# A Fourier-mixing kernel: the second sequence chunk with one plain x pair instead of three, and one sum over xn made by an accumulating DMA

## The chip, the core and the metric

The kernel runs on one core of a Trainium2 chip. A core has TensorE (matmuls, called PE in the profile; PEld is its weight load), VectorE (DVE), ScalarE (ACT), GpSimd (POOL) and SyncE (SP, which here only issues DMAs). The metric is device time in microseconds of one execution: 670.5 us before the change, the median of 3 runs (669.85 to 670.7).

## The reference

x is 2048 x 512. Everything is float32.

```python
xn = _layernorm(x, axis=-1)
a = einsum("bsd,ed->bse", xn, dft_hid_re);  b = einsum("bsd,ed->bse", xn, dft_hid_im)
s = einsum("ts,bse->bte", dft_seq_re, a) - einsum("ts,bse->bte", dft_seq_im, b)
h = einsum("bsd,df->bsf", xn, w1) + b1;  h = relu(h) ** 2      # F = 1792
g = silu(einsum("bsf,fd->bsd", h, w2) + b2)
out = x + s * g
```

The change touches the product of the sequence matrices with the normalised x alone (the kernel does the sequence side first and the hidden side afterwards).

## The kernel before, in words

**Number format.** Every float32 operand is split into a high part (ScalarE copies it into TensorE's format, `split_hi`, L137) and a low part (VectorE subtracts the high part, `split_lo`, L140). A product is three matmul passes: high by high, high by low, low by high (`PASSES`).

**Seven products.** Large matrix products are done block by block as 2 x 2 blocks in seven products instead of eight (Strassen's scheme in Winograd's form). That needs sums of the blocks on both sides: of x, four sums S1 to S4; of the sequence matrix, four sums T1 to T4 (`sums_b`, L299 to L304: three VectorE instructions, 512, 256 and 256 columns wide a partition). A block of the sequence matrix then has 7 parts of 256 columns to split (1792 columns), a plain one 4 (1024).

**Staging of the first part.** The rows of x lie in 16 tiles of 128, two to a "pair" j = 0 to 7. The sequence matrix comes in column chunks of 256, c = 0 to 7; chunk c for pair j is loaded as one block, "block j", into one of three buffers `u`, split into operand `g`, which has two buffers (`ga` for even j, `gb` for odd j). Pairs of x stay in SBUF as operands `xc0` to `xc7`, seven parts each: four raw ones and S1 to S4.

- Chunk 0 goes pair by pair with plain products (`products`, L402, 24 matmuls of 512 columns a pair) while x is being normalised: mean and variance (`ln_stats`, `ln_mean`, `ln_var`), the root, and xn itself by VectorE (`ln_xn`, L242) or by ScalarE (`ln_xn_act`, L253, which needs a small `ln_shift`, L248, by VectorE first). Chunk 0's results are copied out of the PSUM banks by ScalarE (`plain_out`).
- Chunk 1 begins with the pairs of `MIXED` by eight plain products (`plain_step`, 48 matmuls of 256 columns, L391), during which the sums S over xn are formed and split; then come the pairs of `SEVEN` by seven products (42 matmuls, L391). A plain step adds into the same banks as the seven products.
- Chunks 2 to 7 use seven products for all pairs.

**The sums over xn.** `sums(g)` makes S1 to S4 for four pairs at once, in place in the tile `xn32` (L274, 1024 columns a partition each; g = 0 for pairs 0 to 3, g = 1 for 4 to 7). The last of its four steps is an addition, the others are subtractions. `split_sums(j)` then splits the four sums of one pair into `xc`: ScalarE the high part, VectorE the low one.

**The order around the change.** All engines work in the order in which the instructions are written; there is no scheduler. In the loop over seven-product steps n, behind the matmuls of step n are written: the sums of block n + 2 (`step_sums`), the split of block n + 1 (`step_split`), a pair's `split_sums` by the table `SUMS_AT`, the load of block n + 4 (`step_load`), results of the chunk before, and by the table `EARLY` pieces of later work (weights of the hidden side "d", of w1 "v", early operands "y", loads "p"). In the DMA queue of SP the block loads come in the order of use.

Of the kernel before, what the change touches and what calls it, by code (L numbers as in the profile page):

```python
# [11 lines left out]
ALU = mybir.AluOpType  # L12
# [3 lines left out]
NS, ND, NF = S // P, D // P, F // P  # L16
# [3 lines left out]
TC = 512  # L20
NTC = S // TC
WARM = 8, 5
MIXED = 4, 5, 6
SEVEN = 1, 0, 3, 2, 7
SUMS_AT = {1: 7, 2: 4, 3: 5, 5: 6}

REST = NP - 4

# [8 lines left out]


EARLY = {
# [7 lines left out]
}  # L47
LATER = {0: 1, 1: 1, 2: 1, 3: 1, 4: 1}
LATER_1 = {0: 1, 1: 2, 2: 1, 3: 1, 4: 1}
# [82 lines left out]
def fnet_gated_kernel(ctx, tc, x, xt, ct, wd, w1, w2, b1, b2, out):  # L132
# [9 lines left out]
    def split(*parts):  # L142
        split_hi(*parts)
        split_lo(*parts)
# [95 lines left out]
    def ln_xn(j, h):  # L240
        xn32_tile(j, h)
        nc.vector.tensor_scalar(xn32[j][:, h], xr[j][:, h], stats[:, 0, h, j:j + 1], stats[:, 1, h, j:j + 1],  # L242
                                op0=ALU.subtract, op1=ALU.mult)
# [25 lines left out]
    def sums(g):  # L269


        s = xn32[ND * g, "tile"].rearrange("p j h (b n) -> p j (h b) n", b=2)
        for to, a, b, op in ((3, 1, 3, ALU.subtract), (1, 1, 0, ALU.subtract), (0, 3, 0, ALU.subtract), (2, 2, 0, ALU.add)):
            nc.vector.tensor_tensor(s[:, :, to], s[:, :, a], s[:, :, b], op=op)  # L274
            yield

    def split_sums(j):
        s = xn32[j].rearrange("p h (b n) -> p (h b) n", b=2)
        split(XC[j][:, S2:S1 + 1, HI, :], XC[j][:, S2:S1 + 1, LO, :], s)
# [9 lines left out]
    def plain_parts(c, j, hs=slice(0, 2)):  # L289
        if (c, j) not in part:  # L290
            part[c, j] = operand_buf("g" + "ab"[j % 2], f"g{c}_{j}", 0 if c or j == NJ - 1 else 3 if j in TURNED else 1, (2, 4, CW))
        g, r = part[c, j], raw[c, j]
        s = slice(2 * hs.start, 2 * hs.stop)
        return g[:, HI, s], g[:, LO, s], r[:, s]
# [43 lines left out]
    def step_sums(n):  # L338
        if n < len(steps):
            u = raw[steps[n]]  # L340
            sums_b(u[:, 4:8], u)

    def step_split(n):
        if n < len(steps):
            s = steps[n]
            u = raw.pop(s)
            g = part[s] = buf("g" + "ab"[s[1] % 2], [P, 2, 7, CW], f"g{s[0]}_{s[1]}", F32R)
            split(g[:, HI], g[:, LO], u[:, 1:8])
# [48 lines left out]
    def products(j, h):  # L397

        for a_, b_ in PASSES:
            for k in range(ND):  # L400
                w = XC[j][:, RAW[h][k // 2], a_, k % 2 * P:(k % 2 + 1) * P]
                nc.tensor.matmul(accs[k], w, part[0, j][:, b_, 2 * h:2 * h + 2],  # L402
                                 start=j == 0 and h == 0 and (a_, b_) == (HI, HI),
                                 stop=j == NJ - 1 and h == 1 and (a_, b_) == (LO, HI))
# [23 lines left out]
    def go(*names):  # L428


        for v in names:
            if v[0] == "h" and int(v[1:]) >= NTC * NP:
                continue
            if v not in making:
                making[v] = makers[v[0]](int(v[1:]))
            next(making[v])
# [115 lines left out]
    split_hi(*g)  # L552
    for h in range(2):
        products(0, h)
    side = sums(0), sums(1)
    load_c(0, 3)
    load_x(4)
    for j in range(1, NJ):
        ln_rstd(j)
        if j == 1:  # L560
            ln_hi(j, 0)
            ln_shift(j)
            ln_xn_act(j, 0)
            ln_mean(j + 1, 1)
            split_lo(*plain_parts(0, j, one))
            ln_xn(j, 1)
            split_hi(*xc_parts(j, 1))
            split_lo(*xc_parts(j, 0))
            split_lo(*plain_parts(0, j, two))
        else:  # L570
            for h in range(2):
                ln_xn(j, h)
                split_hi(*xc_parts(j, h))
            split_lo(*g)
            split_lo(*xc_parts(j, 0))
        load_c(*order[j + 3])
        if j in (1, 3, 4):
            load_x({1: 5, 3: 6, 4: 7}[j])
        if j + 1 < NJ:
            ln_stats(j + 1)  # L580
            if j > 1:
                ln_mean(j + 1, 1)
            ln_var(j + 1, 1)
            ln_root(j + 1)
        split_lo(*xc_parts(j, 1))
        if j == NJ - 1:
            next(side[0])
        for h in range(2):
            products(j, h)
        g = plain_parts(*order[j + 1])  # L590
        split_hi(*g)
        if j == NJ - 1:
            next(side[0])
        if j == 2:
            nc.sync.dma_start(b1s, b1)
            nc.sync.dma_start(b2s, bcast(b2, D))
# [6 lines left out]
    def plain_out(k):  # L603
        to = plain[k // 2].rearrange("p (i m d t) -> p d m i t", i=2, m=2, d=2)[:, k % 2]
        copy(to, accs[k].rearrange("p (m i t) -> p m i t", m=2, i=2))

    def some(steps_, n):
        for _ in range(n):
            next(steps_)

    for i, j in enumerate(MIXED):
        if i == 0:
            some(side[0], 2)
            some(side[1], 1)
            split(*plain_parts(1, MIXED[1]))
            split_sums(0)
            split_sums(1)
            for k in range(ND):
                plain_out(k)
            for k in range(2):  # L620
                nc.sync.dma_start(PQD[0][:, k].rearrange("p k n -> p (k n)"), plain[k])
        elif i == 1:
            step_sums(0)
            split(*plain_parts(1, MIXED[2]))
            split_sums(2)
            some(side[1], 1)
        else:
            step_sums(1)
            some(side[1], 1)
            step_split(0)  # L630
            split_sums(3)
            go("d0")
        plain_step(j)
        load_c(*order[NJ + i + 4])

# [2 lines left out]
    for n, s in enumerate(steps):  # L638
        c, j = s
        if c > 1 and j == 0:  # L640
            ms = {}
        for k, tag in banks(c).items():
            if k not in ms:
                ms[k] = bank(tag, f"m{k}_{c}")
        g = part.pop(s)
        for p in FIRST if j == 0 and c > 1 else ORDER:
            a, b = PRODUCTS[p]
            mm(ms[p], XC[j][:, a], lambda b_: g[:, b_, b], (c > 1 and j == 0) or (not n and p in (1, 5, 6, 7)), s in LAST)
        step_sums(n + 2)
        step_split(n + 1)  # L650
        if n == 0:
            some(side[1], 1)
        elif n in SUMS_AT:
            split_sums(SUMS_AT[n])
        if n == 0:
            e = buf("e", [P, 2048], "c1")
            copy(chunk_part(e)(C22), halves(ms[Z]))
        step_load(n + 4)
        if closing:
            some(closing, (LATER_1 if c == 2 else LATER).get(j, 0))  # L660
            if j in (3, 4):
# [582 lines left out]
```

## Time and profile before

| | |
|---|---|
| median of 3 runs | 670.5 us |
| profiled execution | 669.43 us |
| its span, first to last instruction | 667.7 us |
| TensorE busy | 662.3 us (99%), 5599 matmuls |
| VectorE busy | 610.7 us (91%), 847 instructions |
| ScalarE busy | 382.1 us (57%), 516 instructions |
| GpSimd busy | 8.8 us (1%), 11 instructions |
| granted TensorE clock | 0.999 |

The span leaves out what lies around the program in one execution (669.43 against 667.7). Rows of a timeline give the start in us from the span's start, the length, engine, source line, operation, output <- inputs with shapes, and in brackets the engine's idle time before it and what ended that. Rows of groups give the count, the total busy time in us, the mean of one in ns, and the idle time ahead. Rows of windows give, behind the stretch, the busy us of PE, PEld, DVE, ACT and POOL with their instruction counts, then the clock and the share of the DMA engines. Matmul lengths overlap; what counts is the distance from one start to the next.

### The profile page before, as it was taken

What the parts mean: (1) busy time and instruction counts of PE and PEld (TensorE: products, weight loads), DVE (VectorE), ACT (ScalarE), POOL (GpSimd) and SP (SyncE); (2) the same over time, 40 slices, a digit from 0 to 9 for tenths busy, and PEclk for the clock granted to TensorE, in tenths of its full rate; (3) what the DMA queues carried; (4) which work ended last, traced back from release to release, by engine and by line L of the source; (5) the groups of instructions that cost most, each with busy time, mean ns of one, the idle gap of its engine ahead of it and who ended that gap; (6) DMA issues with size and microseconds to landing.
All of it is one profiled execution on the core that took longest, in us unless ns stands there. A gap on an engine that the chain in (4) does not pass through costs nothing.

```text
span 667.7 us, 13533 instructions
## 1 busy us (share of the span) xinstructions
PE 662.3 (99%) x5599; PEld 650.9 (97%) x5599; DVE 610.7 (91%) x847; ACT 382.1 (57%) x516; POOL 8.8 (1%) x11
## 2 busy tenths in 40 slices
PE   9999999999999999999999999999999999999997
PEld 6889999999999999999999999999999999999997
DVE  7999999999999999999999979887878889999997
ACT  6855554545545363635465357878778865454451
POOL 0000000000000000000000000000000000101010
PEclk9999999999999999999999999999999999999999
DMA  8634334858668865889588557675845866767676
GB/s 293 228 113 171 121 100 138 290 180 288 220 213 281 303 249 191 296 308 336 198 299 264 180 194 292 209 281 177 299 160 208 339 233 199 203 209 199 212 205 158
DMA packets 52605, 150.85 MB, mean 226 GB/s; under 512 B 5056, under 2 KB 19648, under 8 KB 51904
## 3 DMA queue, kind: packets, MB, share of 16 engines
q1 hardware_dynamic: 44432, 129.28, 57.7%
q10 hardware_dynamic: 6208, 18.88, 7.1%
q0 software_dynamic: 1904, 1.84, 1.9%
q8 instruction: 44, 0.72, 0.4%
q14 instruction: 17, 0.14, 0.1%
HBM read 101.98 MB, written 47.99 MB: 225 GB/s over the span
## 4 chain that ended last, share of the span: by engine, by line
PE 94%; DVE 5%; issue 1%; ACT 0%; DMA 0%; DVEq 0%
PE m L391 40%; PE m_o L909 14%; PE r_B L803 13%; PE r_A L803 9%; PE pq_b L402 5%; PE r_C L803 4%; PE r_D L803 4%; PE pq_bb L402 2%; DVE g L140 1%; PE warm L529 1%; DVE z L959 1%; DVE z L359 1%; DVE z L1159 0%; DVE hr L311 0%; DVE z L964 0%
## 5 line engine op out<-in xcount | busy, mean ns | idle before, releaser
L391 PEld LDWEIGHTS m<-g,xc 128*128 128x128 f32 x2370 | 269.0, 188 | 0.1
L391 PE MATMUL m<-g,xc 128*128 128x256 f32 x2370 | 269.1, 276 | 0.0
L137 ACT ACTIVATE g<-u 128x1792 fp32r<-128x1792 f32 (+2 forms) x65 | 102.3, 1574 | 132.7 <-PE m L391 65.2
L140 DVE TENSOR_TENSOR g<-u,g 128x1792 fp32r<-128x1792 f32 (+2 forms) x66 | 120.9, 1832 | 6.8 <-ACT g L137 6.2
L909 PE MATMUL m_o<-w,g 128*128 128x256 f32 x882 | 100.5, 276 | 0.0
L909 PEld LDWEIGHTS m_o<-w,g 128*128 128x128 f32 x882 | 100.3, 188 | 0.0
L137 ACT ACTIVATE g<-hr 128x1792 fp32r<-128x1792 f32 (+2 forms) x31 | 48.2, 1566 | 40.2 <-PE m_o L909 16.8
L803 PE MATMUL r_B<-xT,w 128*128 128x256 f32 x504 | 66.6, 276 | 0.0
L803 PEld LDWEIGHTS r_B<-xT,w 128*128 128x128 f32 x504 | 61.5, 188 | 0.0
L140 DVE TENSOR_TENSOR g<-hr,g 128x1792 fp32r<-128x1792 f32 (+2 forms) x31 | 56.7, 1838 | 2.9 <-ACT g L137 2.8
L803 PE MATMUL r_A<-xT,w 128*128 128x256 f32 x336 | 43.1, 276 | 0.0
L402 PE MATMUL pq_b<-g,xc 128*128 128x512 f32 x144 | 40.9, 391 | 0.0
L803 PEld LDWEIGHTS r_A<-xT,w 128*128 128x128 f32 x336 | 40.4, 188 | 0.2 <-DVE xT L140 0.2
L301 DVE TENSOR_TENSOR u<-u 128x512 f32<-128x512 f32 x53 | 36.3, 684 | 0.7 <-DMA u<-in_ct 0.6
L803 PE MATMUL r_B<-wdp,yg 128*128 128x256 f32 x288 | 35.8, 276 | 0.0
L803 PEld LDWEIGHTS r_B<-wdp,yg 128*128 128x128 f32 x288 | 34.1, 188 | 0.0
L909 PE MATMUL m_last<-w,g 128*128 128x256 f32 x294 | 33.5, 276 | 0.0
L909 PEld LDWEIGHTS m_last<-w,g 128*128 128x128 f32 x294 | 33.4, 188 | 0.0
L402 PEld LDWEIGHTS pq_b<-g,xc 128*128 128x128 f32 x144 | 26.8, 188 | 6.6 <-ACT g L137 0.7
L140 DVE TENSOR_TENSOR yg<-yraw,yg 128x1792 fp32r<-128x1792 f32 x13 | 26.2, 2020 | 0.6 <-ACT yg L137 0.6
L137 ACT ACTIVATE yg<-yraw 128x1792 fp32r<-128x1792 f32 x13 | 22.2, 1708 | 5.4 <-DVE yraw L315 4.5
L303 DVE TENSOR_TENSOR u<-u 128x256 f32<-128x256 f32 x53 | 22.5, 425 | 1.8
(185 smaller groups left out, 837.2 us busy)
## 6 DMA issues: line engine op xcount, KB each, us to landing
u<-in_ct SPq DMA_DIRECT2D x63, 512.0 KB, 4.1
hd<-h ACTq DMA_DIRECT2D x28, 512.0 KB, 4.4
hr<-hd SPq DMA_DIRECT2D x28, 512.0 KB, 3.8
wdp<-wdd SPq DMA_DIRECT2D x8, 896.0 KB, 7.1
yraw<-pqd SPq DMA_DIRECT2D x13, 512.0 KB, 5.2
pqd<-c SPq DMA_DIRECT2D x12, 512.0 KB, 5.2
w<-w1d SPq DMA_DIRECT2D x6, 896.0 KB, 7.8
y<-y ACTq DMA_DIRECT2D x8, 512.0 KB, 5.1
```

The costliest lines, as they stand in the source:

```text
L137: nc.scalar.activation(hi, src, AF.Copy)
L140: nc.vector.tensor_tensor(lo, src, hi.bitcast(F32), op=ALU.subtract)
L301: nc.vector.tensor_tensor(t[:, 0:2], r[:, 0:1].to_broadcast([P, 2, 256]), r[:, 1:3], op=ALU.add)
L303: nc.vector.tensor_tensor(t[:, 2], t[:, 1], r[:, 1], op=ALU.add)
L359: nc.vector.tensor_tensor(part_(to), m, part_(frm), op=op)
L391: nc.tensor.matmul(ps[:, d], w[:, a_, d * P:(d + 1) * P], halves(mv(b_)), start=first and d == 0 and (a_, b_) == (HI, HI), stop=last and ( ...
L402: nc.tensor.matmul(accs[k], w, part[0, j][:, b_, 2 * h:2 * h + 2], start=j == 0 and h == 0 and (a_, b_) == (HI, HI), stop=j == NJ - 1 and ...
L529: nc.tensor.matmul(warm, zeros[:, 0:P], zeros, start=True, stop=True)
L803: nc.tensor.matmul(self.region(REGION[k]), w, mv, start=i == 0 and k in (1, 7), stop=i == len(ops) - 1, skip_group_check=True)
L909: nc.tensor.matmul(m[:, i * 256:(i + 1) * 256], ready[n][:, a_, H_SLOT[a], i * P:(i + 1) * P], W2[p][:, b_, b], start=p == 0 and i == 0 an ...
L959: nc.vector.tensor_tensor(e[:, k, w], e[:, k, w], fin[c][k // 2][:, k % 2, w], op=ALU.mult)
```

## The change

Four things are done.

1. Chunk 1 has one plain pair (4) instead of three (4, 5, 6); pairs 5 and 6 move to the seven-product steps, which now go 1, 0, 3, 2, 5, 6, 7.
2. Of the four sums over xn, the addition is no longer a VectorE instruction but two accumulating DMAs on GpSimd's queue, SBUF to SBUF, for two pairs each (twice, for g = 0 and 1).
3. The last pair (7) is normalised by ScalarE (`ln_shift` and `ln_xn_act`) instead of VectorE.
4. The order of sums, splits and copies around this is rewritten, and the tables `SUMS_AT` and `EARLY` are renumbered.

```diff
-MIXED = 4, 5, 6
-SEVEN = 1, 0, 3, 2, 7
-SUMS_AT = {1: 7, 2: 4, 3: 5, 5: 6}
+MIXED = 4,
+SEVEN = 1, 0, 3, 2, 5, 6, 7
+SUMS_AT = {0: 3, 1: 2, 2: 5, 3: 6, 4: 7, 5: 4}
...
 EARLY = {
-    (2, 2): ("d0",), (2, 3): ("d0",), (2, 5): ("d0", "d1"), (2, 6): ("d0",), (3, 0): ("d1",), (3, 1): ("d1",),
+    (1, 2): ("d0",),
+    (2, 0): ("d0",), (2, 2): ("d0",), (2, 3): ("d0", "d1"), (2, 5): ("d0",), (2, 6): ("d1", "d1"), (3, 0): ("d1", "d2"),
...
         s = xn32[ND * g, "tile"].rearrange("p j h (b n) -> p j (h b) n", b=2)
-        for to, a, b, op in ((3, 1, 3, ALU.subtract), (1, 1, 0, ALU.subtract), (0, 3, 0, ALU.subtract), (2, 2, 0, ALU.add)):
-            nc.vector.tensor_tensor(s[:, :, to], s[:, :, a], s[:, :, b], op=op)
+        for to, a, b in ((3, 1, 3), (1, 1, 0), (0, 3, 0)):
+            nc.vector.tensor_tensor(s[:, :, to], s[:, :, a], s[:, :, b], op=ALU.subtract)
             yield
+        for q in (slice(0, 2), slice(2, 4)):
+            nc.gpsimd.dma_start(s[:, q, 2], s[:, q, 0], accum_op=ALU.add)
+        yield
...
+            if j == NJ - 1:
+                ln_shift(j)
+                next(side[0])
             for h in range(2):
-                ln_xn(j, h)
+                (ln_xn_act if j == NJ - 1 else ln_xn)(j, h)
                 split_hi(*xc_parts(j, h))
...
         if j == NJ - 1:
-            next(side[0])
+            some(side[0], 3)
         for h in range(2):
             products(j, h)
         g = plain_parts(*order[j + 1])
         split_hi(*g)
-        if j == NJ - 1:
-            next(side[0])
...
     for i, j in enumerate(MIXED):
-        if i == 0:
-            some(side[0], 2)
-            some(side[1], 1)
-            split(*plain_parts(1, MIXED[1]))
-            split_sums(0)
-            split_sums(1)
-            for k in range(ND):
-                plain_out(k)
-            for k in range(2):
-                nc.sync.dma_start(PQD[0][:, k].rearrange("p k n -> p (k n)"), plain[k])
-        elif i == 1:
-            step_sums(0)
-            split(*plain_parts(1, MIXED[2]))
-            split_sums(2)
-            some(side[1], 1)
-        else:
-            step_sums(1)
-            some(side[1], 1)
-            step_split(0)
-            split_sums(3)
-            go("d0")
+        some(side[1], 4)
+        step_sums(0)
+        step_split(0)
+        plain_out(2)
+        plain_out(0)
+        split_sums(1)
+        plain_out(1)
+        plain_out(3)
+        for k in range(2):
+            nc.sync.dma_start(PQD[0][:, k].rearrange("p k n -> p (k n)"), plain[k])
+        step_sums(1)
+        split_sums(0)
         plain_step(j)
         load_c(*order[NJ + i + 4])
...
         step_sums(n + 2)
         step_split(n + 1)
-        if n == 0:
-            some(side[1], 1)
-        elif n in SUMS_AT:
+        if n in SUMS_AT:
             split_sums(SUMS_AT[n])
```

How this moves instructions. Names: `u1_1` is block 1 of chunk 1, `g1_1` its split operand, `xc1` pair 1 of x, `xn32_0` and `xn32_4` the tiles of xn with the sums of pairs 0 to 3 and 4 to 7.

VectorE before, from the low half of block 4 (the first plain pair) to block 1's sums:

```order
L140 TENSOR_TENSOR g1_4_546<-u1_4_428,g1_4_546 128x1024
L274 TENSOR_TENSOR xn32_0_184<-xn32_0_184 128x4x256 x2
L274 TENSOR_TENSOR xn32_4_374<-xn32_4_374 128x4x256
L140 TENSOR_TENSOR g1_5_557<-u1_5_473,g1_5_557 128x1024
L140 TENSOR_TENSOR xc0_121<-xn32_0_184,xc0_121 128x4x256
L140 TENSOR_TENSOR xc1_126<-xn32_0_184,xc1_126 128x4x256
L301 TENSOR_TENSOR u1_1_550<-u1_1_550 128x512
```

and the same place now:

```order
L141 TENSOR_TENSOR g1_4_551<-u1_4_428,g1_4_551 128x1024
L275 TENSOR_TENSOR xn32_4_374<-xn32_4_374 128x4x256 x3
L305 TENSOR_TENSOR u1_1_473<-u1_1_473 128x512
L307 TENSOR_TENSOR u1_1_473<-u1_1_473 128x256
L308 TENSOR_TENSOR u1_1_473<-u1_1_473 128x256
L141 TENSOR_TENSOR g1_1_566<-u1_1_473,g1_1_566 128x1792
L141 TENSOR_TENSOR xc1_126<-xn32_0_184,xc1_126 128x4x256
```

The sums over pairs 0 to 3 have moved ahead of block 4, the three sums of pairs 4 to 7 stand together, and block 1's low half follows its own sums directly.

VectorE now, from there to the low half of block 0, the operand of the second seven-product pair:

```order
L305 TENSOR_TENSOR u1_0_520<-u1_0_520 128x512
L307 TENSOR_TENSOR u1_0_520<-u1_0_520 128x256
L308 TENSOR_TENSOR u1_0_520<-u1_0_520 128x256
L141 TENSOR_TENSOR xc0_121<-xn32_0_184,xc0_121 128x4x256
L305 TENSOR_TENSOR u1_3_554<-u1_3_554 128x512
L307 TENSOR_TENSOR u1_3_554<-u1_3_554 128x256
L308 TENSOR_TENSOR u1_3_554<-u1_3_554 128x256
L141 TENSOR_TENSOR g1_0_685<-u1_0_520,g1_0_685 128x1792
```

Between the low halves of blocks 1 and 0 there now stand two pairs' splits of sums and the sums of two blocks; before, one of each (pair 3's split and block 3's sums).

ScalarE now, from the last pair of chunk 0 to the high half of block 0 (`plain` are the copies of chunk 0's results, `pq0_bb` the bank in which the first of the seven products will add up):

```order
L254 ACTIVATE xn32_4_374<-x7_383,small_129,stats_68 128x512
L138 ACTIVATE xc7_125<-xn32_4_374 128x2x256
L138 ACTIVATE g1_4_551<-u1_4_428 128x1024
L138 ACTIVATE g1_1_566<-u1_1_473 128x1792
L148 ACTIVATE plain1_557<-pq0_bb_132 128x2x2x128
L148 ACTIVATE plain0_556<-pq0_b21_130 128x2x2x128
L138 ACTIVATE xc1_126<-xn32_0_184 128x4x256
L148 ACTIVATE plain0_556<-pq0_b32_131 128x2x2x128
L148 ACTIVATE plain1_557<-pq0_b31_133 128x2x2x128
L138 ACTIVATE xc0_121<-xn32_0_184 128x4x256
L138 ACTIVATE g1_0_685<-u1_0_520 128x1792
```

Block 1's high half comes ahead of all four copies; before, the four copies, the sums of pairs 0 and 1 and two plain blocks came ahead of it.

More of the change, by code (lines that the diff above doesn't have):

```diff
@@ L554, in fnet_gated_kernel, with some @@
         products(0, h)
+    def some(steps_, n):
+        for _ in range(n):
+            next(steps_)
     side = sums(0), sums(1)
@@ L605, in plain_out @@
         copy(to, accs[k].rearrange("p (m i t) -> p m i t", m=2, i=2))
-    def some(steps_, n):
-        for _ in range(n):
-            next(steps_)
     for i, j in enumerate(MIXED):
-        if i == 0:
-            some(side[0], 2)
-            some(side[1], 1)
-            split(*plain_parts(1, MIXED[1]))
-            split_sums(0)
-            split_sums(1)
-            for k in range(ND):
-                plain_out(k)
-            for k in range(2):
-                nc.sync.dma_start(PQD[0][:, k].rearrange("p k n -> p (k n)"), plain[k])
-        elif i == 1:
-            step_sums(0)
-            split(*plain_parts(1, MIXED[2]))
-            split_sums(2)
-            some(side[1], 1)
-        else:
-            step_sums(1)
-            some(side[1], 1)
-            step_split(0)
-            split_sums(3)
-            go("d0")
+        some(side[1], 4)
[10 more added lines that the diff above has]
+        split_sums(0)
         plain_step(j)
```

12 rows, old and new, of the table EARLY are left out of this document.

## The prediction

> **What bounds the kernel now.** I read the page first, then the list of waits on TensorE, then one window of the timeline engine by engine.
>
> ```profile
> span 667.7 us, 13533 instructions
> PE 662.3 (99%) x5599; PEld 650.9 (97%) x5599; DVE 610.7 (91%) x847; ACT 382.1 (57%) x516; POOL 8.8 (1%) x11
> L391 PE MATMUL m<-g,xc 128*128 128x256 f32 x2370 | 269.1, 276 | 0.0
> PE warm L529 <- DVE idle L525: 1.2, 1, 1.2
> 50.91 59.33 PE L391 MATMUL m<-g,xc 128*128 128x256 f32 x522
> 67.00:91.00 24.00, 24.00 (x214) 24.00 (x213) 22.59 (x26) 13.99 (x13) 0.00 (x0) 1.00 0.32 107
> ```
>
> The fourth row is the whole list of TensorE's waits: once warm it waits for nobody. The fifth is its timeline from the first product of the second chunk: 522 matmuls in one piece, so one starts every (59.33 - 0.276) / 521 = 0.1133 us. A plain pair of x has 48 of them, 5.44 us; a seven-product pair has 42, 4.76 us. The last row is the stretch after it (PE, PEld, DVE, ACT, POOL, clock): TensorE is full, and VectorE has 22.59 of 24 us. So TensorE sets the time, but only while VectorE, nearly as full, delivers. Any matmul removed is won, any late operand is lost.
>
> **What is removed.** Pairs 5 and 6 go from plain to seven products: 2 x 6 = 12 matmuls, 12 x 0.1133 = 1.36 us. That is the whole gain to be had.
>
> **What it costs VectorE.** The rows that price it (timeline of VectorE; start, length, what):
>
> ```profile
> 40.65 0.16 DVE L233 SCALAR_TENSOR_TENSOR stats<-small 128x2 f32<-128x2 f32 x1
> 40.85 1.00 DVE L242 TENSOR_SCALAR xn<-x,stats 128x512 f32<-128x512 f32 x2
> 41.77 1.22 DVE L140 TENSOR_TENSOR g<-u,g 128x1024 fp32r<-128x1024 f32 x1
> 42.90 1.29 DVE L140 TENSOR_TENSOR xc<-xn,xc 128x512 fp32r<-128x512 f32 x2
> 44.10 2.49 DVE L274 TENSOR_TENSOR xn<-xn 128x1024 f32<-128x1024 f32 x2
> 46.60 1.23 DVE L140 TENSOR_TENSOR g<-u,g 128x1024 fp32r<-128x1024 f32 x1
> 47.74 3.61 DVE L274 TENSOR_TENSOR xn<-xn 128x1024 f32<-128x1024 f32 x3
> 61.12 0.69 DVE L301 TENSOR_TENSOR u<-u 128x512 f32<-128x512 f32 x1
> 61.84 0.43 DVE L303 TENSOR_TENSOR u<-u 128x256 f32<-128x256 f32 x1
> 62.30 0.42 DVE L304 TENSOR_TENSOR u<-u 128x256 f32<-128x256 f32 x1
> 62.64 1.22 DVE L274 TENSOR_TENSOR xn<-xn 128x1024 f32<-128x1024 f32 x1
> 63.78 2.03 DVE L140 TENSOR_TENSOR g<-u,g 128x1792 fp32r<-128x1792 f32 x1
> 65.73 1.22 DVE L140 TENSOR_TENSOR xc<-xn,xc 128x1024 fp32r<-128x1024 f32 x1
> 66.86 0.69 DVE L301 TENSOR_TENSOR u<-u 128x512 f32<-128x512 f32 x1
> ```
>
> From start to start: a 1024-wide operation 1.14 (46.60 to 47.74), or 2.49 / 2 = 1.25, say 1.27 with its gap, where the next one reads its result; the low half of 1792 columns 1.95 (63.78 to 65.73); of four sums 1.13; the three sums of a block 1.52 (61.12 to 62.64). Work: pairs 5 and 6 each trade a plain low half (1.14) for a block's sums and a 1792 low half (3.47), +4.7 for both; two additions over xn leave for the accumulating DMAs, -2.4; the last pair's normalisation leaves for ScalarE, 41.77 - 40.85 = -0.92. In all VectorE gets some 1.4 us more. The amount is not the matter, the place is: the work that must stand before the first seven-product pair had three plain pairs as cover (16.3 us from 50.91 to 67.23, where its low half was done at 63.78 + 2.03 = 65.81); now it has one, until 56.35.
>
> The ScalarE rows that join in (timeline, then groups by form):
>
> ```profile
> 40.06 1.06 ACT L137 ACTIVATE g<-u 128x1024 fp32r<-128x1024 f32 x1
> 45.51 1.06 ACT L137 ACTIVATE g<-u 128x1024 fp32r<-128x1024 f32 x1 [2.92 <-PE pq_b L402]
> 53.97 1.06 ACT L147 ACTIVATE plain<-pq_b 128x512 f32<-128x512 f32 x2
> 54.92 0.60 ACT L147 ACTIVATE plain<-pq_bb 128x512 f32<-128x512 f32 x1
> 62.05 1.71 ACT L137 ACTIVATE g<-u 128x1792 fp32r<-128x1792 f32 x1 [3.43 <-issue]
> L253 ACT ACTIVATE xn<-x,small,stats 128x512 f32<-128x512 f32 x3 | 2.4, 808 | 0.8 <-DVE small L248 0.8
> L137 ACT ACTIVATE xc<-xn 128x512 fp32r<-128x512 f32 x13 | 7.5, 624 | 2.9 <-DVE xn L242 2.9
> ```
>
> **The chain, in the new order.** Up to 40.85 nothing differs. VectorE then does the shift of the last pair (two elements; 0.07 to 0.20 by the 0.16 of the first row, I take 0.10): 40.95. First sum of side 0: 42.09. Low half of block 7: 43.23. Of pair 7's two low halves the second waits for ScalarE, which from 41.12 does 0.81 + 0.62 + 0.81 + 0.62 = 2.86 us, to 43.98; this hides in ScalarE's 2.92 us pause before 45.51. VectorE starts that half at 44.00 and goes on at 44.60. Sums two and three of side 0: 45.87, 47.01 (the third ends at 47.09). Low half of block 4: 48.15. Three sums of side 1: 49.42, 50.69, 51.83. Sums of block 1: 0.72 + 0.46 + 0.42 = 1.60, done 53.43.
>
> ScalarE can only now take block 1's high half, 53.46 to 55.17 (1.71); VectorE has nothing it may do meanwhile and starts the low half at 55.20 (63.76 to 63.78 in the rows above is the hand-over), done at 57.23. The plain pair ends at 50.91 + 48 x 0.1133 = 56.35. The next matmul (high by high) can run, the one behind it, due at 56.46, needs the low half: 57.28. **First wait: 0.82 us.** The bank it starts in is copied out first (about 55.1 to 55.7), and the high half of pair 1's sums follows at about 56 to 57, so neither is later than this.
>
> VectorE continues: low half of pair 1's sums 57.15 to 58.28, sums of block 0 to 59.80, low half of pair 0's sums to 60.93, sums of block 3 to 62.45, and only then block 0's low half, done at 62.45 + 2.03 = 64.48. TensorE wants it 42 x 0.1133 = 4.76 us after 57.28, at 62.04, and gets it at 64.53. **Second wait: 2.49 us.** The 1.52 us for block 3 stand ahead of it because the sums are written before the split, as they were before, where the cover was there.
>
> After that VectorE needs 1.95 + 1.13 + 1.52 = 4.60 us a pair against 4.76: block 3's low half is done at 69.08, due 69.29, and the margin grows by 0.16 each pair. So no third wait. The shifted table of early weight work only places the same pieces some steps earlier; VectorE's margin hides it. Were that gone, this is the price:
>
> ```profile
> 286.00:294.00 8.00, 8.00 (x73) 8.00 (x72) 7.20 (x13) 4.14 (x3) 0.00 (x0) 1.00 0.94 330
> 294.00:302.00 8.00, 8.00 (x70) 7.97 (x69) 7.90 (x10) 2.69 (x2) 0.00 (x0) 1.00 0.82 294
> 292.23 0.69 DVE L301 TENSOR_TENSOR u<-u 128x512 f32<-128x512 f32 x1 [0.62 <-DMA u<-in_ct]
> ```
>
> A transfer 0.62 us late for VectorE left TensorE 3 matmuls short in the next 8 us, about 0.34. In the new kernel TensorE comes 2 us later there, so this may vanish (0 to -0.34); and a hole may leave TensorE slower for some us behind it as here (0 to 0.33 for each of two). I take zero for the pair, near their sum.
>
> **The accumulating DMAs.** Before, POOL's queue does the like only in the last stage, from HBM:
>
> ```profile
> 571.39 1.33 POOL L947 DMA_DIRECT2D z<-in_x  x1 [570.95 <-DVE z L959]
> DMA to landing us min/median/max: 4.6/5.0/7.6
> 573.12 2.02 DVE L140 TENSOR_TENSOR g<-hr,g 128x1792 fp32r<-128x1792 f32 x1
> u<-in_ct SPq DMA_DIRECT2D x63, 512.0 KB, 4.1
> ```
>
> Each is 256 KB, as there. Issued at 47.1, the one for pairs 0 and 1 lands at 52.1 by the median, 54.7 by the longest; ScalarE asks for it at 56, so 1.3 us are left at worst and it costs nothing. Its companion lands some 1.3 us later (POOL's 1.2 to 1.33 for each) and is asked for after 61; side 1's are issued at 51.9 and asked for after 68. Block loads stay in SP's order, one step further on, and are asked for about 5.7 us after their buffer comes free (low half of one block to the sums three blocks on), against 4.1.
>
> **Sum.** 0.82 + 2.49 - 1.36 = +1.95 us: on the profiled execution 669.43 to 671.4. The median shown stands 1.07 above that execution, so I set **672.4 us** against 670.5, or 0.29% more. By the open terms (shift 0.1 either way, after-effects -0.34 to +0.66, the durations to 1% of a 23 us chain) the forecast's own range is 671.8 to 673.2. A measurement of this kernel can tell about 0.2%, 1.34 us, from no change.
>
> **Rivals.** *VectorE is in time* and the 1.36 us are won: 669.1. It needs the chain to block 0's low half 2.5 us shorter, and to block 1's 0.8. For it: part of VectorE's time in the old stretch was waiting for ScalarE, so the old order had slack in it:
>
> ```profile
> 52.20 1.22 DVE L140 TENSOR_TENSOR g<-u,g 128x1024 fp32r<-128x1024 f32 x1 [0.84 <-ACT g L137]
> 57.70 1.23 DVE L140 TENSOR_TENSOR g<-u,g 128x1024 fp32r<-128x1024 f32 x1 [0.49 <-ACT g L137]
> ```
>
> Against it: every instruction in my chain is measured and only 1.8 us of the 23.6 are waits. Chance 0.08.
>
> *A part comes back*: both waits come, but the loss near 295 us is gone (-0.34) and the open terms fall the cheap way (-0.3 for the shift and the chain's 1%): 1.95 - 0.64 = +1.3, 671.8 or a little under, within the 0.2%. For it: the 3 missing matmuls above, which the later TensorE no longer has to lose. Against it: a hole may cost something behind it too, as that one did. Chance 0.18.
>
> [...] Chance 0.10.
> [...]
>
> **How the numbers follow.** Forecast 0.64, in time 0.08, part back 0.18, late accumulate 0.10. Faster by over 0.2% is the first rival alone, 0.08. The second, and the lowest edge of the forecast (about 0.06), lie within 0.2%: 0.24. Slower: 0.68. The range 670.4 to 674.2 leaves out the first rival and most of the third.
>
> **What would show it.** Right: TensorE's list of waits gains two rows in the second chunk, near 56.5 (about 0.8, released by the low half of block 1, 1792 wide) and near 62 (about 2.5, by block 0's); VectorE has an idle of about 1.8 behind ScalarE before block 1's low half, and its timeline runs gapless from there; the first matmul of the first chunk-2 pair comes 1.9 to 2.0 us later than before. Wrong: a wait on the DMA at pair 1's sums (third rival); no gap of TensorE near 62 (first); a third gap in the pairs 3, 2, 5, 6, 7, or one at the moved weight work in chunks 2 to 7, which would add to the loss.

## The result, and the profile after

The changed kernel takes 674.2 us (median of 6, 672.13 to 675.95) against 670.6 for the kernel before (6, 669.85 to 671.52): 1.0055 times, 95% interval 1.0036 to 1.0074. Later runs of the changed kernel, each beside runs of the kernel before, gave +2.8, +3.0 and +3.2 us. Slower, as forecast; but by 2.8 to 3.6 us and not by 1.95.

The profiled execution is the fastest of the six (672.13, span 670.3 against 667.7). From its page, the cost group and the list of TensorE's waits, the rows for this part:

```profile
span 670.3 us, 13529 instructions
PE 661.4 (99%) x5587; PEld 650.0 (97%) x5587; DVE 611.6 (91%) x850; ACT 384.8 (57%) x518; POOL 13.7 (2%) x15
L395 PE MATMUL m<-g,xc 128*128 128x256 f32 x2358 | 268.8, 276 | 2.8 <-DVE g L141 2.8
PE m L395 <- DVE g L141: 2.8, 2, 2.2
```

Twelve matmuls are gone (2370 to 2358), and TensorE, which waited for nobody, waits twice for a low half from VectorE. (The list's other rows, 1.2 and 0.6 us, lie in the first 8 us.) Where, by the timelines of TensorE and of VectorE (start, length, what, idle before it):

```profile
50.99 5.73 PE L395 MATMUL m<-g,xc 128*128 128x256 f32 x49
57.33 5.03 PE L395 MATMUL m<-g,xc 128*128 128x256 f32 x42 [0.61 <-DVE g L141]
64.57 45.63 PE L395 MATMUL m<-g,xc 128*128 128x256 f32 x397 [2.21 <-DVE g L141]
```

```profile
55.25 2.03 DVE L141 TENSOR_TENSOR g<-u,g 128x1792 fp32r<-128x1792 f32 x1 [1.82 <-ACT g L138]
62.50 2.02 DVE L141 TENSOR_TENSOR g<-u,g 128x1792 fp32r<-128x1792 f32 x1
```

A matmul's own 0.276 us overlaps the next by 0.163, so a gap of 0.61 sets TensorE back by 0.61 + 0.163 = 0.77 us and one of 2.21 by 2.37. Forecast: 0.82 and 2.49; VectorE idle 1.8 behind ScalarE, here 1.82; the low halves done at 57.23 and 64.48, here 57.28 and 64.52. The places and sizes are those of the prediction. 3.14 - 1.36 = 1.78; the span grew by 2.6. Two stretches show more loss, and a third shows one that is gone (the windows' columns as in the prediction: stretch, then PE, PEld, DVE, ACT, POOL, clock). Of the changed kernel:

```profile
64.57:76.00 11.43, 11.43 (x97) 11.43 (x98) 11.22 (x14) 5.15 (x5) 1.22 (x1) 1.00 0.62 154
120.00:160.00 40.00, 40.00 (x351) 40.00 (x350) 38.15 (x48) 19.58 (x18) 0.00 (x0) 1.00 0.73 243
294.00:302.00 8.00, 8.00 (x73) 8.00 (x72) 7.42 (x10) 4.36 (x3) 0.00 (x0) 1.00 0.85 298
```

and of the kernel before:

```profile
120.00:160.00 40.00, 40.00 (x355) 40.00 (x355) 38.36 (x50) 21.51 (x19) 0.00 (x0) 1.00 0.74 254
```

11.43 us at 0.1133 are 101 matmuls, and 97 started: 0.4 us of slower pace right behind the second wait, without any wait. Between 120 and 160 there are 4 fewer than before, another 0.45. Against that stands the loss near 295 us, 0.30 of the kernel before by the starts of its matmuls, which is gone: 73 matmuls from 294 to 302 us, where the kernel before had 70. By the same starts, the first matmul of chunk 2 comes at 93.50 us against 91.04, 2.46 later where the prediction named 1.9 to 2.0, and chunks 2 to 7 add 0.18. That is this execution; the median lies 2 us above it, and the question became what the other executions lose.

### The profile page after: what moved, and what is told of

Read it like the earlier page. It is cut to its first block, busy times and chain, and to the rows that moved or that the text cites. A ratio compares the mean times of both kernels' runs of the same rounds, so it can differ in the third digit from the quotient of the medians.

```text
span 670.3 us, 13529 instructions
## 1 busy us (share of the span) xinstructions
PE 661.4 (99%) x5587; PEld 650.0 (97%) x5587; DVE 611.6 (91%) x850; ACT 384.8 (57%) x518; POOL 13.7 (2%) x15
## 4 chain that ended last, share of the span: by engine, by line
PE 93%; DVE 4%; ACT 1%; DMA 1%; issue 1%; SPq 0%; DVEq 0%; ACTq 0%
PE m L395 38%; PE m_o L903 15%; PE r_B L797 13%; PE r_A L797 9%; PE r_C L797 4%; PE r_D L797 4%; PE pq_b L406 4%; PE m_last L903 4%; PE pq_bb L406 1%; DVE xn L275 1%; DMA u<-in_ct 1%; ACT g L138 1%; DVE g L141 0%; DVE z L1153 0%; DVE xc L141 0%
## 5 line engine op out<-in xcount | busy, mean ns | idle before, releaser
L395 PEld LDWEIGHTS m<-g,xc 128*128 128x128 f32 x2358 | 268.4, 188 | 3.3 <-DVE g L141 3.2
L395 PE MATMUL m<-g,xc 128*128 128x256 f32 x2358 | 268.8, 276 | 2.8 <-DVE g L141 2.8
L141 DVE TENSOR_TENSOR g<-u,g 128x1792 fp32r<-128x1792 f32 (+2 forms) x66 | 122.4, 1855 | 6.1 <-ACT g L138 5.6
```

The costliest lines, as they stand in the source:

```text
L141: nc.vector.tensor_tensor(lo, src, hi.bitcast(F32), op=ALU.subtract)
L395: nc.tensor.matmul(ps[:, d], w[:, a_, d * P:(d + 1) * P], halves(mv(b_)), start=first and d == 0 and (a_, b_) == (HI, HI), stop=last and ( ...
```

## The experiments

**Is it the accumulating DMA?** By theory V the order of VectorE's work sets both waits; by theory D a late accumulate does or adds to them. Three edits, and the changed kernel once more (after_again). no_add leaves the fourth of the four sums out, with nothing in its place:

```diff
-        for q in (slice(0, 2), slice(2, 4)):
-            nc.gpsimd.dma_start(s[:, q, 2], s[:, q, 0], accum_op=ALU.add)
```

dve_add lets VectorE add it at that place:

```diff
-        for q in (slice(0, 2), slice(2, 4)):
-            nc.gpsimd.dma_start(s[:, q, 2], s[:, q, 0], accum_op=ALU.add)
+        nc.vector.tensor_tensor(s[:, :, 2], s[:, :, 2], s[:, :, 0], op=ALU.add)
```

acc_early makes the subtractions over pairs 0 to 3 sooner, so that their transfers start sooner:

```diff
-                next(side[0])
+                some(side[0], 2)
...
-        if j == NJ - 1:
-            some(side[0], 3)
+        some(side[0], {5: 1, 6: 1, 7: 0}.get(j, 0))
```

> The changed kernel once more, to see in a profile what most of its executions look like: the profiled one took 672.1 us, the median is 674.2. Two theories for the missing 2 us. Theory V (VectorE's chain is all): the two waits of TensorE near 56.5 and 62 us are larger in the common execution, with VectorE slower or its block loads late, 674.2 again. Theory D (the accumulating DMA is late): in the profiled execution the first one was issued at 47.7 and landed at 55.4, only 0.7 us before ScalarE could use it (56.07); in the common execution it lands at 57.5 to 58, ScalarE's high half of pair 1's sums starts only then, and TensorE waits some 2 us more. If the profile kept is a fast execution again (672.1), it shows nothing.

> The changed kernel without the fourth sum over xn: the four accumulating DMAs are left out and nothing takes their place (that sum is left unmade, so the product that uses it is of other data); everything else stands as it was. VectorE's and ScalarE's chains are unchanged. Theory D: 672.1 us, with TensorE's waits of 0.8 and 2.4 us as in the profiled execution, and executions within 0.5 us of each other. Theory V: 674.2 as the changed kernel, same spread (672 to 676).

> The changed kernel with the fourth sum made by VectorE again, as a fourth step where the other three stand (1.14 to 1.27 us each, one for pairs 0 to 3 before block 4's low half, one for pairs 4 to 7 before block 1's sums); no accumulating DMA. The chain ahead of block 1's low half gets 2.5 us longer, the waits of TensorE become about 3.2 and 2.4. Theory D: 672.1 + 2.5 = 674.6 us with little spread, no slower than the changed kernel by more than 0.5. Theory V: 674.2 + 2.5 = 676.7 with the same spread.

> The changed kernel with the three subtractions over pairs 0 to 3 two sums earlier (one behind pair 5, one behind pair 6, the third at the start of pair 7), so that the accumulating DMA is issued about 3.5 us earlier, at some 44 us. VectorE's work ahead of block 1 is the same in sum. Theory D: the landing no longer counts, 672.3 us and little spread. Theory V: 674.2, as the changed kernel.

Measured, against 670.27: after_again 673.05 (ratio 1.0025 to 1.0056), no_add 673.51 (the same interval), acc_early 673.12 (1.0026 to 1.0056), dve_add 675.87 (1.0047 to 1.0098). TensorE's waits in the profile of no_add:

```profile
PE m L393 <- DVE g L141: 2.8, 2, 2.2
```

Without any accumulating DMA the same two waits stand, and the time is the same: D falls, and with it the third rival, a late accumulate. Doing the sum on VectorE costs 2.8 us more than the DMA does (675.87 against 673.05), so the DMA is worth its 2.4 us of VectorE's time, and VectorE's chain is the bound. (Only four executions of dve_add were taken. In its profile the gaps are 1.65, 1.19 and 2.03 us; the first ends with ScalarE's copy of the bank, which stands behind block 1's high half and so behind VectorE's sums.) acc_early gained nothing; its profile showed instead a block load that came late for VectorE (2.02 us of idle at 125.73), a loss that is not in the prediction.

**Is it the table of early weight work, or the order?** The new table sets a weight's store and the next weight's load ahead of block loads on SP's queue (theory E). old_early is the changed kernel with the table of before, plus one piece, `(1, 2): ("d0",)`; new_early is the kernel before with the new table and without its `go("d0")`. one_plain and two_plain keep the old table and change the order: one_plain has one plain pair. In it the sums of block 1 stand ahead of the sums over pairs 4 to 7, those of block 0 ahead of block 1's low half, the sums over pairs 0 to 3 are spread over pairs 5 to 7, and ScalarE normalises pairs 5 to 7 instead of 7 alone, so VectorE has less to do as well. From its edit:

```diff
-                (ln_xn_act if j == NJ - 1 else ln_xn)(j, h)
+                (ln_xn_act if j in (5, 6, 7) else ln_xn)(j, h)
...
-        some(side[1], 4)
+        some(side[1], 1)
...
```

two_plain keeps two plain pairs:

```diff
-MIXED = 4,
-SEVEN = 1, 0, 3, 2, 5, 6, 7
+MIXED = 4, 5
+SEVEN = 0, 1, 2, 3, 6, 7
...
```

> The changed kernel with the old table of early weight work (its first entry, the load of the first weight, stands in the second chunk as in the new one). Theory E: the new table sends a 768 KB store and a 512 KB weight load into SP's queue ahead of a block load of chunk 2, that load lands 6 to 8 us after its issue instead of 4, VectorE waits 0.6 to 2.0 us for it and TensorE loses 0 to 2.1 us between 127 and 135 us; this is what the executions differ by. Then the old table gives 672.2 us here against 673.2 for the changed kernel, with no wait of VectorE on a block load between 110 and 130, and the two waits of TensorE near 57 and 63 us (3.3 us together) as they were. Theory N (the executions differ by something else, the same for the kernel before): 673.2 as the changed kernel.

> The kernel before with the new table of early weight work alone; its matmuls and the second chunk stay as they were (one piece, the first weight's load, moves to where the new table has it). Theory E: VectorE waits on a block load between 115 and 126 us, TensorE loses 0.3 to 1.5 us there, 670.6 to 671.8 against 670.3. Theory N: 670.3, no such wait.

> A version that should not have the two waits: one plain pair, accumulating DMAs, and the old table; the sums of blocks 1 and 0 are written ahead of the sums over pairs 4 to 7, so that ScalarE has block 1's operand early and VectorE has other work meanwhile; the last three pairs are normalised by ScalarE, and the sums over pairs 0 to 3 stand behind pairs 5, 6 and 7, which issues the accumulating DMA some 3 us earlier. By VectorE's chain with the durations of the rows: a wait of 0.2 us near 56 and of 1.0 us near 61, so 1.2 - 1.36 = -0.2 us against before plus 0 to 0.3 behind the holes: 670.2 us, 2.9 us faster than the changed kernel. If the waits are not set by VectorE's order: no faster than 672.2.

> Two plain pairs (4, 5), then seven products for 0, 1, 2, 3, 6, 7 (so that the two operand buffers still alternate), old table, accumulating DMAs, sums of block 0 ahead of the split of block 5. Six matmuls fewer than before, -0.68 us; by VectorE's chain no wait at the start of the seven products and 0.3 us at the end of the chunk: 670.0 us, -0.3 against before. If the accumulating DMA lands 2 us later than in the profiled execution, +0.9.

Measured, against 670.54: old_early 673.48 (1.0028 to 1.0058), new_early 670.72 (0.9996 to 1.0013), one_plain 670.23 (0.998 to 1.0009), two_plain 670.82 (0.9999 to 1.002). TensorE's waits in the profile of one_plain:

```profile
PE m L395 <- DVE g L141: 0.8, 2, 0.5
```

One plain pair is possible at the old time: with the same twelve matmuls gone, the other order leaves gaps of 0.28 and 0.51 us where there were 0.61 and 2.21. So the seven-product form does not bring the two waits. That the order of VectorE's work alone removes them isn't shown, because one_plain also takes two normalisations off VectorE, 0.92 us each by the prediction's rows; what ties the waits to the order is the predicted chain, which the changed kernel's timeline follows to 0.1 us. one_plain wins nothing either: 12 matmuls pay for two small waits, and none of these versions beats the kernel before measurably. two_plain, expected at 670.0, has gaps of TensorE of 0.2 us near 92 and of 0.8 near 222. The table alone costs the kernel before nothing that shows. In the changed kernel old_early took what theory N had (673.2) and over a microsecond more than theory E's 672.2, and its profile shows something that neither had named. The windows of old_early:

```profile
62.00:66.00 4.00, 1.97 (x17) 1.76 (x16) 3.93 (x6) 4.00 (x5) 0.00 (x0) 1.00 0.93 218
66.00:70.00 4.00, 4.00 (x24) 4.00 (x23) 3.93 (x6) 0.12 (x1) 1.22 (x1) 0.57 0.79 192
70.00:76.00 6.00, 6.00 (x53) 6.00 (x53) 4.71 (x6) 2.65 (x2) 0.00 (x0) 1.00 0.26 90
66.50:69.80 3.30, 3.30 (x18) 3.30 (x17) 3.23 (x5) 0.00 (x0) 1.22 (x1) 0.50 0.84 201
```

Behind the second wait TensorE is busy all the time, waits for nobody, and starts 24 matmuls where 35 fit: the granted clock, 1.00 in the windows around it, is 0.57 over these 4 us and 0.50 in the stretch from 66.5 to 69.8 alone. From the starts of the matmuls, 15 in a row come at 0.213 us, 3.2 us in all. Each loses 0.1, 1.5 together. An execution with such a stretch has a mean granted clock 0.0025 lower (3.4 x 0.5 / 673, an estimate), so it can be told from the clock that each execution reports: 0.997 or less.

**Does the wait itself bring the half clock?** Fill it. 18 matmuls of no use, into a bank that is free there, behind the first seven-product pair; the copy that frees the bank moves a few steps ahead into an idle of ScalarE (not in the lines shown). fill_old has the old table too. swap leaves the matmuls as they are and cuts the wait by order alone:

```diff
+        if n == 1:
+            fill = bank("ba", "fill")
+            for _ in range(18):
+                nc.tensor.matmul(fill[:, 0:256], XC[4][:, 0, 0, 0:P], XC[4][:, 0, 0], start=True, stop=True)
...
```

```diff
-        step_sums(n + 2)
-        step_split(n + 1)
+        if not n:
+            step_split(n + 1)
+            step_sums(n + 2)
+        else:
+            step_sums(n + 2)
+            step_split(n + 1)
```

> The changed kernel with 18 matmuls of no use (one raw pair by itself, 256 wide, into the bank that C22's first sums have left) put on TensorE between the first and the second seven-product pair, where it waits 2.4 us for block 0's low half; 18 x 0.1133 = 2.04 us, so they fill the wait and delay nothing. ScalarE's copy out of that bank moves ahead of block 0's high half, into an idle of 1.05 us. Nothing of the computation is left out. Clock theory: the profiles of the changed kernel differ in one thing above all, a stretch of 3.4 us right behind the second wait in which TensorE's granted clock is half (15 matmuls at 0.213 us, 1.7 us lost); it is in some executions only, those whose mean granted clock is 0.996 or 0.997, and it follows from the idle itself. Then, with the idle filled, no execution has a mean clock under 0.998, and the median falls from some 673.3 to 672.7 (670.4 + 1.95 + up to 0.4 for slower matmuls behind the hole). Rival: the low clock comes from elsewhere (the chip, or VectorE's and ScalarE's load) and only the time that VectorE needs counts: then about a third of the executions still has 0.996 to 0.997 and the median stays at 673.3.

> The same 18 matmuls, and the table of early weight work as it was before (with one more piece, the first load, in place of what the third plain pair did). Table theory: with the clock out of the way, the new table costs about 1.1 us, because it sets the first weight's store and the second's load ahead of a block load and VectorE no longer has slack there: fill_old 671.8, about 0.9 to 1.1 below fill_new, with no wait of VectorE for a block load near 123. Rival, the table costs nothing here either (as it cost nothing in the kernel before): fill_old and fill_new within 0.4 us of each other.

> The changed kernel with one pair of steps of VectorE exchanged: block 0's low half ahead of the three sums of block 3. The prediction's own arithmetic: the second wait falls by 1.52, to about 0.9, and the third pair stays in time by some 0.2; so 0.8 + 0.9 - 1.36 = +0.35 of 670.4, 670.8, plus 0 to 1.1 for the table: 671.3. By the clock theory an idle of 0.9 us is too short for the half clock, so no execution under 0.998. If instead the long wait has another cause than VectorE's order, it stays near 2.4 us and the time near 673.3.

> The changed kernel unchanged, on the same chip as the three others, as their base: 673.3, with a mean granted clock of 0.996 or 0.997 in about a third of its executions (by the clock theory), and these about 1.7 us above the others.

Measured, against 670.39: after_third 673.41 (1.0026 to 1.006), fill_new 672.36 (1.0015 to 1.0038), fill_old 672.22 (1.0014 to 1.004), swap 673.8 (1.003 to 1.0067). Three of the six executions of after_third had 0.996 or 0.997; of the 23 with the wait filled, and of the 6 of swap, none. One execution of fill_new, the one with the profile, took 3846 us with every matmul at about a sixth of its speed (L395's 2358 matmuls busy for 1559.0 us, against 268.8 in the changed kernel's page); I can't explain it and leave it out.

swap missed its time. TensorE's timeline of it:

```profile
57.53 5.21 PE L395 MATMUL m<-g,xc 128*128 128x256 f32 x42 [0.59 <-DVE g L141]
64.12 5.05 PE L395 MATMUL m<-g,xc 128*128 128x256 f32 x42 [1.37 <-DVE g L141]
70.24 4.98 PE L395 MATMUL m<-g,xc 128*128 128x256 f32 x40 [1.07 <-DVE g L141]
```

Three gaps, and more in all than two had (3.03 against 2.82). I had taken the third pair's due time from the kernel with the long second wait; with that wait shorter the third pair is due sooner as well, and the 1.52 us of block 3 stand ahead of its low half just as they stood ahead of block 0's. Exchanging two pieces of a chain that is too long moves the wait, it doesn't shorten the chain. Each gap sets TensorE back by 0.28 us more than its length (0.163 of overlap, and the second start behind it comes 0.11 late), so the three cost 3.86 and the sum would be 3.86 - 1.36 = +2.5. Of the +3.4 measured, 0.9 is not accounted for.

**What do executions at full clock still lose?** Those of the changed kernel lay 2.7 above the kernel before, not 1.95. Four more runs, among them the table once more and swap with the old table (swap_old).

> The changed kernel, base of the next three. Clock theory: a mean granted clock of 0.996 or 0.997 in some 9 of 22 executions as so far, these some 2 us above the others; median 673.4, the others alone 673.0.

> The changed kernel with the table of early weight work as before (and the one load in place of the third plain pair's). Table theory: late block loads of the new table near 118 and 125 us (0.9 and 1.6 us on VectorE in the last profile of the changed kernel, 1.4 us of them on TensorE) are what remains above the sum; then the executions at full clock lie at 671.9, about 1.1 below the changed kernel's at full clock, and the profile has no such wait there. Rival, no difference (as with the wait filled, 672.22 against 672.36): within 0.4 of the changed kernel at the same clock.

> The wait filled with 18 matmuls, the new table: no execution under 0.998, as in the 12 before; median 672.3, that is, the sum of the prediction without anything behind the hole (before + 1.95). Its profile shows the second wait gone to 0.2 to 0.4 us, TensorE's pitch behind it not slower than 0.1133 (0.36 us lost at 64 to 76 otherwise), and, by the table theory, the same late block loads near 118 and 125; where it has none, the difference of 0.8 to the changed kernel at full clock is the slower pitch and those loads.

> The exchange of block 0's low half and block 3's sums with the old table. The exchange alone gave three waits (0.87, 1.65, 1.34 us, 3.86 in all, since the third pair is due 0.8 us sooner than I reckoned) for the two of the changed kernel (0.87 and 2.49), no execution under 0.998, and 673.8 in the middle. Table theory: with the old table 672.6 (670.4 - 1.36 + 3.86 less 0.3), 1.2 below; rival: 673.8 again, so the spread at full clock has nothing to do with the table.

Measured, against 670.19: after_fourth 673.36 (1.0024 to 1.0052), old_early_again 672.94 (the same interval), fill_new_again 672.5 (1.0016 to 1.0041), swap_old 672.96 (1.0024 to 1.0049). The profiled executions of the two unfilled kernels have the low mean clock again (after_fourth 0.997, old_early_again 0.996), that of fill_new_again doesn't (0.999). Windows of after_fourth:

```profile
60.00:64.60 4.60, 2.67 (x23) 2.47 (x21) 4.53 (x7) 4.37 (x4) 0.00 (x0) 1.00 1.01 265
64.60:65.30 0.70, 0.60 (x2) 0.60 (x3) 0.70 (x2) 0.70 (x2) 0.00 (x0) 0.54 0.37 56
65.30:68.70 3.40, 3.40 (x20) 3.40 (x20) 3.33 (x5) 0.59 (x1) 1.22 (x1) 0.59 0.76 195
68.70:72.00 3.30, 3.30 (x32) 3.30 (x31) 3.13 (x5) 0.71 (x1) 0.00 (x0) 1.00 0.70 180
```

TensorE's timeline, and windows, of fill_new_again:

```profile
57.66 5.10 PE L395 MATMUL m<-g,xc 128*128 128x256 f32 x41 [0.57 <-DVE g L141]
62.59 2.31 PE L645 MATMUL fill<-xc 128*128 128x256 f32 x18
64.74 10.43 PE L395 MATMUL m<-g,xc 128*128 128x256 f32 x89
```

```profile
62.00:66.00 4.00, 4.00 (x35) 3.92 (x34) 3.94 (x5) 3.64 (x4) 0.01 (x1) 1.00 0.80 194
66.00:70.00 4.00, 4.00 (x37) 4.00 (x37) 3.93 (x5) 0.07 (x1) 1.22 (x1) 1.00 0.83 190
```

The operand comes at about the same moment (64.74 against 64.57), so the filled kernel still loses the time of the wait, but nothing that these windows show behind it: the full pace is there at once. All executions together, as time above the middle of the kernel before that was run beside them:

| | executions | clock 0.997 or less | these | the others | all |
|---|---|---|---|---|---|
| changed kernel, 4 runs | 34 | 16 | +3.8 | +2.7 | +3.2 |
| with the old table, 2 runs | 20 | 12 | +3.6 | +1.6 | +2.8 |
| wait filled, new table, 2 runs | 23 | 0 | | +2.3 | +2.3 |
| wait filled, old table | 12 | 0 | | +1.8 | +1.8 |
| swap, swap_old | 18 | 0 | | +3.4, +2.8 | |
| kernel before, run beside these | 113 | 0 | | 0 | |

Filled, both tables: +2.02 (35 executions); unfilled, both tables: +3.08 (54). The difference is 1.06 us, 0.5 to 1.6 by resampling the executions; with the changed kernel's own table alone it is 0.9. That is the price, on the middle of the executions, of all that stands behind the wait. Most of it is the half clock, by an estimate: 1.6 us in 28 of the 54 executions are 0.8 on average. The unfilled executions at full clock lie 0.4 above the filled ones (2.4 against 2.0), which resampling (-0.4 to 1.0) can't tell from nothing.

The table stays open. In all three comparisons the old one is lower at full clock (2.7 against 1.6, 2.3 against 1.8, 3.4 against 2.8), but resampling gives 0.2 to 1.8 for the first and nothing distinguishable for the other two, and the expected 1.1 came only once. That a block load which lands late costs time in some executions is shown. VectorE's timeline of after_third, an execution at full clock:

```profile
118.55 0.69 DVE L305 TENSOR_TENSOR u<-u 128x512 f32<-128x512 f32 x1 [0.86 <-DMA u<-in_ct]
124.78 0.69 DVE L305 TENSOR_TENSOR u<-u 128x512 f32<-128x512 f32 x1 [1.56 <-DMA u<-in_ct]
```

and TensorE's there, with its window:

```profile
128.39 7.85 PE L395 MATMUL m<-g,xc 128*128 128x256 f32 x64 [1.14 <-DVE g L141]
120.00:160.00 40.00, 38.86 (x337) 38.53 (x337) 37.31 (x48) 19.62 (x18) 0.00 (x0) 1.00 0.66 230
```

TensorE has a third gap, and starts 18 matmuls fewer than in the kernel before, 2 us. The profile of acc_early, with the same table, has such a gap too (1.58 us at 129.33, behind the late load at 125.73). The profiles of the old table in the changed kernel have no such wait there. But the filled kernel with the old table had a late load too, elsewhere (at 234 us, 1.09 us of VectorE's idle), so the table moves and perhaps adds late loads; it isn't their only cause.

## Why the prediction was right and where it was wrong

- **What bounds the kernel, and what is removed**: right. TensorE waits for nobody before, each late operand is lost in full, and 12 matmuls are 1.36 us.
- **The chain in the new order**: right to 0.1 us at every point that it named, and so are both waits (0.77 and 2.37 for 0.82 and 2.49). one_plain shows from the other side that they go with the order and amount of VectorE's work and not with the seven-product form.
- **No third wait in the pairs behind**: right in the four profiles of the changed kernel as far as chunk 1 goes. swap shows how close it was: the same work in another order has three.
- **After-effects of the holes**: this is the step that failed. The prediction said "a hole may leave TensorE slower for some us behind it as here (0 to 0.33 for each of two)" and "I take zero for the pair". Behind the second wait TensorE ran at half clock in 16 of 34 executions (by their mean clock of 0.997 or less), for some 3.4 us, by the windows of old_early and after_fourth, and at a loss of 1.5 to 1.6 us where a profile caught it, and in profiles at full clock it lost up to 0.4 through a pace some 3% slower (in after, after_third and no_add; hardly any in after_again, acc_early and dve_add). So the term taken as zero measured 1.06 us on the middle of the executions. With the wait filled the time is near the prediction's sum: +1.95 forecast, +2.02 measured for both tables together, +2.3 with the changed kernel's own table and +1.8 with the old one. That the first agrees to 0.1 is in part luck, since late block loads, which the sum has at nothing, are in it. The price came from a row near 295 us, the only hole in the trace before, and TensorE shows no gap there (8.00 of 8.00 us busy, 3 matmuls short); nothing in it could show what a hole of 2.4 us does. But the bound of 0.33 was then not one for a hole that long, and the range for the forecast's own case (671.8 to 673.2, where the terms it names reach 673.4) should not have stood on it.
- **The table, "VectorE's margin hides it"**: it doesn't hide it in every execution. The margin starts at 0.2 us behind the second wait and grows by 0.16 a pair, and block loads that were late by 0.9 and 1.6 us came through to TensorE in after_third, as the third gap in chunk 2 that the prediction named as a sign of being wrong, and cost 2 us. How much of such lateness is the table's stays open.
- **The loss near 295 us may vanish (0 to -0.34)**: it did in the profiled execution, -0.30. With the old table old_early lost time there again (a gap of 0.27 us at 300.77, behind a load that was 1.05 us late), so TensorE's coming later isn't enough by itself.
- **The accumulating DMAs cost nothing**: right; no_add takes as long. But "its companion lands some 1.3 us later" was wrong, as the last section shows; it cost nothing because the first sums of its two pairs, pair 3's, are asked for by ScalarE only at 61.71, 2.3 us behind its landing. The first transfer landed at 55.3, 0.6 later than the longest that the prediction allowed.
- **Rivals**: *VectorE is in time* fell, both waits are there. *A part comes back*: its first half came in the profiled execution, and was outweighed. *Late accumulate*, 0.10: no run shows one that delays TensorE; without any accumulating DMA (no_add) the same two waits stand, and the time is 673.51 against 673.05 with them (after_again).

## What to carry to other kernels

Here a wait of a saturated TensorE of 2.0 to 2.2 us had a second price behind it, 1.06 us on the middle of the executions: price a wait by its length, and then look in the runs for what the clock does behind it (0.997 or less in 34 of 75 executions with such a wait, in none of 18 with waits up to 1.4 us). Where such a wait can't be removed, it can be filled: matmuls of no use gave that 1.06 us back here. Exchanging two of VectorE's steps made three gaps of 0.6 to 1.4 us, which kept the clock too, but the executions were no faster for it (+3.4 and +2.8). Before moving two pieces of a chain against each other, compute the due times again from the new first wait, since a chain that is too long keeps its deficit in any order.

## What the runs showed of the hardware

**Half clock behind a gap of 2 us.** Five kernels have a gap of TensorE of 2.0 to 2.2 us between stretches at full pace (the changed one, old_early, no_add, dve_add, acc_early). Of their 75 executions 34 had a mean clock of 0.997 or less. Three of the nine that were profiled are of that kind (old_early 0.997, old_early_again 0.996, after_fourth 0.997); the other six have 0.999 or 1.0. The 18 executions of swap and swap_old, with gaps up to 1.4 us, had 0.999 or 1.0 as well.

The windows above show the slow stretch of two of the three. In old_early the granted clock is 0.50 from 66.5 to 69.8, with matmuls at 0.213 instead of 0.113 us, and 0.57 over 66 to 70: some 3.4 us (4.0 x 0.43 / 0.50), from about 1.5 us after TensorE had resumed at 64.92. In after_fourth it is 0.54 and 0.59 in the two windows behind the gap, from 64.60 on and so with the first matmul, and 1.00 from 68.70 on; by an estimate with old_early's 0.50 these are 3.4 us too (0.7 x 0.46 / 0.50 + 3.4 x 0.41 / 0.50). Why only some executions have it was not shown: the gap has the same length in both kinds, 2.03 us in old_early and after_fourth, and 2.03 in after_again, dve_add and acc_early and 2.21 in after and no_add, all five at 0.999 or 1.0.

**The second and third accumulating DMA started when the one before had landed.** Three rows of GpSimd's timeline in the changed kernel, and the time from issue to landing of all four:

```profile
47.72 1.33 POOL L278 DMA_DIRECT2D xn<-xn  x1 [47.28 <-DVE xn L275]
55.62 1.23 POOL L278 DMA_DIRECT2D xn<-xn  x1 [6.57 <-ACT g L138]
59.69 1.21 POOL L278 DMA_DIRECT2D xn<-xn  x1 [2.83 <-ACT xc L138]
DMA to landing us min/median/max: 3.8/5.0/7.6
```

The first two were written one behind the other, and the second started at 55.62, when the first had landed (47.72 + 7.6 = 55.3), not 1.3 us behind it. The third came 0.3 us after the second's landing (55.62 + 3.8 = 59.4) as well, at 59.69. The first, the longest, left ScalarE's split of pair 1's sums at 56.07 only 0.7 us. Why it is so wasn't tried.
